# A state-space layer beside attention with memory rows: V of the memory rows turned by transposing DMA instead of TensorE

## The chip, the cores and the metric

The kernel runs on one core of one Trainium2 chip. Times are microseconds (us) of device time of one execution; the median of three executions is given. The profile was taken by the hardware profiler on one execution; its span runs from the first to the last instruction.

## The reference

Two independent layers read a sequence of 2048 tokens with 1024 features each, and their outputs are put side by side. Part A is a diagonal complex state-space recurrence. Part B is attention over segments of 32 tokens, 64 segments one after the other; each segment sees 8 memory rows, which are the output of the segment before.

```python
for s in range(n_seg):                                   # 64 segments
    h = jnp.concatenate([mem, x[:, s*32:(s+1)*32]], axis=1)   # 8 memory rows and 32 tokens
    q, k, v = (einsum('btd,dhe->bhte', h, W) for W in (Wq, Wk, Wv))   # 32 heads of 128
    p = softmax(where(mask, einsum('bhqe,bhke->bhqk', q, k) * scale, -1e9))
    o = einsum('bhte,hed->btd', einsum('bhqk,bhke->bhqe', p, v), Wo)
    mem, out = o[:, :8], o[:, 8:]
```

## The kernel before, in words

The segments of part B depend on each other only through the memory rows. The kernel guesses those rows (method `guess`), computes all segments at once with them, and checks at the end that the guess was good enough; if not, a slow exact loop (`general`) runs. So there are 73 memory rows beside the 2048 tokens: NM = 73, of which NMX = 7 belong to the first segment and NTL = 66 to the others.

The work goes through four stages.

1. **Stage one** (lines 999 to 1061). `warm` (line 960) issues short TensorE matmuls on zeros while the first data arrive. `v_x` (line 464) makes V = x Wv of the tokens, 512 tokens and four heads (a block, `hb`, of eight) at a time, and stores it to the DRAM tensor `b_vx`; for the first 512 tokens, x comes as rows and is turned by TensorE (`turn_x0`, line 404), whose results DVE or ACT copies out of PSUM. Part A's recurrence (`stage1`) is interleaved with it. In this stage the instructions of TensorE and of SP's queue stand in the written order (`k.pin`, line 1001).
2. **Stage two** (lines 1067 to 1093). Part A's output product, 32 halves of a tile of 128 tokens, 16 matmuls of 512 columns each, counted by `i`. Between the halves `guess` runs (until `i` = 23), and then the first two steps of `v_mem` (line 541), for blocks 0 and 1. SP's queue is still in the written order.
3. **Attention** (lines 1096 to 1135). For 16 pairs of heads, `proj` makes Q and K of a pair in 18 steps (16 matmuls of 201 columns for the odd columns in each of two steps, 8 of 480 columns in each of sixteen), and `attention` takes 11 units a pair: scores (`psS`), exponential on ACT, mask on GpSimd, the product with V (`psO` or `psR`, from `att_back`) and the division on DVE. LEAD = 10 projection steps run before the first unit, and the rest is spread between the units. The compiler may reorder here, except where `keep_in_program_order` is called. The steps of `v_mem` for blocks 2 to 7 run at units 4 and 6 of every second pair.
4. **Output product** and the check.

`v_mem` for block `hb` multiplies Wv (the tile `b_wv`, two buffers; the next load of Wv waits until the matmuls are done with the old one) by the 73 guessed rows, which gives V of these rows with the head's 128 features on the partitions (`b_vm`). It has to stand the other way, rows on the partitions. So four TensorE transposes turn it, DVE copies it into a staging tile `b_vst` (line 555), and SP stores 7 rows to `b_vx` and 66 rows to `b_vt` in DRAM (lines 557 and 558). Each head has 128 columns of V and then columns of ones, which give the softmax's sum.

`load_v` (line 619) brings V of a pair of heads from `b_vx` and `b_vt` into one of two buffers `b_v`. For the first two pairs it first fills 29 partitions (rows 99 to 127) with zeros from DRAM, by a DMA of 22 x 29 pieces. The load for pair 0 is issued by `att_init` (line 690), the load for pair hp + 1 at unit 2 of pair hp. Lines 625 and 627 keep the zeros and the body in program order on SP.

Of the kernel before, what the change touches and what calls it, by code (L numbers as in the profile page):

```python
# [9 lines left out]
BF16 = mybir.dt.bfloat16  # L10
# [16 lines left out]
HB = 8; HP = 16  # L27
# [7 lines left out]
NMX = 7  # L35
NM = NTL + NMX
# [3 lines left out]
EW = E + 8  # L40
# [13 lines left out]
class Pinned:  # L54


    def __init__(self, k, name, eng):
        self.k, self.name, self.eng = k, name, eng
# [278 lines left out]
class PartB:  # L337
    def __init__(self, k, x, mem0, Wq, Wk, Wv, Wo, out):
        self.k = k
        self.x, self.mem0, self.out = x, mem0, out  # L340
        self.Wf = [w.rearrange("(c p) h e -> p c (h e)", p=128) for w in (Wq, Wk, Wv)]
        self.Wo = Wo.rearrange("h e d -> e h d")
        self.vx = [k.drp.tile([NSLOT, 4 * EW], BF16, name=f"b_vx{i}") for i in range(HB)]
        self.vt = [k.drp.tile([NTL, 4 * EW], BF16, name=f"b_vt{i}") for i in range(HB)]
        self.on = [k.drp.tile([T, 1024], BF16, name=f"b_on{i}") for i in range(4)]
        self.tn = [k.drp.tile([NR, 1024], BF16, name=f"b_tn{i}") for i in range(4)]
        c = k.cst
        self.m0T = c.tile([128, KC, M], BF16, name="b_m0T")
        self.gx = c.tile([128, KC, NM], BF16, name="b_gx")
        self.vmp = c  # L350
        self.xbar = c.tile([128, KC, NSEG], BF16, name="b_xbar")
        self.ogT = c.tile([128, H, NSEG], BF16, name="b_ogT")
        self.accE = c.tile([128, HP * NU], FP32, name="b_accE")
        self.accR = c.tile([128, HP * 2 * NG], FP32, name="b_accR")
        self.flag = c.tile([1, 1], I32, name="b_flag")
# [48 lines left out]
    def turn_x0(self, i):  # L404

        k = self.k
        pt = k.ps("U", (128, 2, KC, 128), BF16)[:, 0, :, :]
        for c in range(KC):
            k.PE.transpose(pt[:, c, :], self.x0[i][:, c * 128:(c + 1) * 128], k.ident[:])
        k.copy("vs"[i // 2], self.xe[:, :, 128 * i:128 * i + 128], pt)  # L410

    def sum_x(self, tmp):

# [50 lines left out]
    def v_x(self, hb, q, w):  # L464

        k = self.k
        Q = k.nc.scalar
        vx = self.vx[hb]
        st = self.next_st()
        first = hb == 0 and q == 0  # L470
        if first:

            ps = [k.ps("P")[:] for _ in range(3)]
            self.turn_x0(0)
            k.warm(6)
            self.turn_x0(1)
            for i, c in ((0, 0), (0, 1), (1, 0), (1, 1)):
                self.v_mm(ps[i], w, i, 128 * c, 128 * c + 128)
            self.turn_x0(2)
            self.v_mm(ps[0], w, 0, 256, 512)  # L480
            self.v_mm(ps[1], w, 1, 256, 512)
            self.turn_x0(3)
            ps.append(k.ps("U", (128, 2, 512))[:, 0, :])
            self.v_mm(ps[2], w, 2)
            self.v_mm(ps[3], w, 3)
        for i in range(4):
            if first:
                p = ps[i]
            else:
                p = k.ps("P")[:]  # L490
                self.v_mm(p, w, 4 * q + i)
            k.copy("v" if first and i % 2 else "s", st[:, i, :, 0:E], p.rearrange("p (h e) -> p h e", h=4))
        s0 = GX + 4 * q * 128
        n = 4 if q < 3 else 3
        Q.dma_start(vx[s0:s0 + n * 128, :].rearrange("(i p) n -> p i n", p=128), st[:, 0:n, :, :].rearrange("p i h e -> p i (h e)"))
        if q == 3:
            sv = st[:, 3, :, :].rearrange("p h e -> p (h e)")
            Q.dma_start(vx[0:64, :], sv[0:64, :])
            Q.dma_start(vx[T - 32:T + 32, :], sv[64:128, :])
# [41 lines left out]
    def v_mem(self, hb, w=None):  # L541
        k = self.k
        w = w or self.load_wv(hb)
        p = k.ps("P")
        for h in range(4):
            for c in range(KC):
                k.PE.matmul(p[:, h * NM:(h + 1) * NM], w[:, c, h * 128:(h + 1) * 128], self.memT[:, c, :], start=(c == 0), stop=(c == KC - 1))
        vm = self.vmp.tile([128, 4, NM], BF16, name="b_vm", bufs=1)
        k.copy("v", vm[:], p[:, 0:4 * NM].rearrange("p (h n) -> p h n", h=4))
        yield  # L550
        pt = k.ps("P", (128, 1024), BF16)
        for h in range(4):
            k.PE.transpose(pt[0:NM, h * 128:(h + 1) * 128], vm[:, h, :], k.ident[:])
        st = self.next_st()
        k.copy("v", st[0:NM, 0, :, 0:E], pt[0:NM, 0:512].rearrange("p (h e) -> p h e", h=4))
        sv = st[:, 0, :, :].rearrange("p h e -> p (h e)")
        k.SP.dma_start(self.vx[hb][64:64 + NMX, :], sv[0:NMX, :])
        k.SP.dma_start(self.vt[hb][:], sv[NMX:NM, :])
        yield


# [397 lines left out]

def warm(k, pool):  # L960

    w = pool.tile([128, 128], BF16, name="a_n", bufs=1)
    k.V.memset(w[:], 0.0)
    p = k.ps("R")

    def more(n):
        for _ in range(n):
            k.PE.matmul(p[:, 0:128], w[:], w[:], start=True, stop=True)
    more(24)
    k.warm = more  # L970


def hint(k):
# [6 lines left out]
def kernel_main(tc, A_x, A_Lre, A_Lim, A_Bre, A_Bim, A_Cre, A_Cim, A_logdt, A_Dskip, B_x, B_mem0, B_Wq, B_Wk, B_Wv, B_Wo, out,  # L980
                force=False, dbg=None):
    with ExitStack() as ctx:
        k = K(tc, ctx)
# [3 lines left out]
        b = PartB(k, B_x, B_mem0, B_Wq, B_Wk, B_Wv, B_Wo, out)  # L987

        def pool(name, side, bufs=2):
            return tc.tile_pool(name=name, bufs=bufs, side=side, reuse_waits="tile")  # L990
# [8 lines left out]
        with pool("p1x", "right") as p1x, pool("p1", "right", 1) as p1:  # L999
            a.tab = a.tmp = a.wp = a.btp = p1  # L1000
            k.pin |= {"PE", "SP"}
            warm(k, p1)
            w0 = b.wl.tile([128, KC, 512], BF16, name="b_wv", bufs=2)
            b.load_wv_part(w0, 0, 0, 128, nc.scalar)
# [5 lines left out]
            wv = {0: w0, 1: b.load_wv(1)}  # L1010
# [17 lines left out]
            for kind, pc, q in order[1:]:  # L1028
# [3 lines left out]
                if kind == "v":  # L1032
                    b.v_x(pc, q, wv[pc])
                    if q == 3:
                        if pc >= 3:
                            b.og(pc, wv[pc])
                        n = (pc + 2) if pc + 2 < PC else (2, 0)[pc + 2 - PC]
# [3 lines left out]
                n = 4 * pc + q  # L1041
# [27 lines left out]
        with pool("p2h", "right") as p2h, pool("p2", "right") as p2:  # L1069
            a.s2_tiles(p2h, p2)  # L1070
            g = b.guess(p2)
            s2 = a.stage2()
            b.wog = []
            a.load_h(1, nc.scalar)
            for i, _ in enumerate(s2):
                if i in (1, 4, 7):
                    n = (2, 0, 1)[(i - 1) // 3]
                    b.og(n, wv[n], "O")
                    if n == 2:
                        wv[1] = b.load_wv(1)  # L1080
                if i in (3, 7, 11, 15):
                    b.load_wog((3, 7, 11, 15).index(i), p2)
                if i in (9, 11, 13, 15, 17, 19, 21, 22):
                    next(g)
                if i == 20:
                    b.load_wqk(0)
                if i == 23:
                    for _ in g:
                        pass
                if i in (26, 28):  # L1090
                    vm = b.v_mem((i - 26) // 2, wv[(i - 26) // 2])
                if 26 <= i < 30:
                    next(vm)


# [15 lines left out]
        for n, (hp, u) in enumerate(at):  # L1111
            if n == 12:
                k.SP.dma_start(wo0[:], b.Wo[:, :, 0:512])
            if hp % 2 == 0 and 2 < hp + 2 < HP:
                if u == 4:
                    vm = b.v_mem(hp // 2 + 1)
                if u in (4, 6):
                    next(vm)
            if hp == 13 and u in (3, 6, 9):
                b.load_o_early(u // 3 - 1)  # L1120
            want = min(18 * HP, LEAD + (n + 1) * 18 // 11)
            while done < want:
                next(pr)
                done += 1
            if done == 18 * HP:
                if first is None:
                    xs.close()
                    b.p4a = ctx.enter_context(pool("p4a", "left", 1))
                    wo1 = b.p4a.tile([128, H, 512], BF16, name="wo1")
                    b.wo = (wo0, wo1)  # L1130
                    b.load_o_early(3)
                    for h in range(0, H, 16):
                        k.SP.dma_start(wo1[:, h:h + 16, :], b.Wo[:, h:h + 16, 512:D])
                    first = b.outproj_first()
                next(first)
# [90 lines left out]
```

## Time and profile before

| what | value |
|---|---|
| median of three executions | 1248.39 us (1248.22 to 1248.77) |
| the profiled execution | 1248.77 us |
| its span, first to last instruction | 1247.0 us |
| instructions | 20164 |
| mean granted TensorE clock | 1.000 |
| SP's DMA queue | 147.95 MB, 293830 packets |

How to read the lines that follow in this document. A group line gives the line of the kernel (often that of a helper, L64 for all TensorE and SP calls), the engine, the operation, what it writes and reads by the program's names (`psP<-b_xe,b_wv` is a matmul into a PSUM tile of tag P that reads `b_xe` and `b_wv`), its shape, how many there are, and durations in ns (least, median, largest). A timeline line gives start and length in us of a run of like instructions. `SPq` is SP's queue of DMA issues; its length is the time in which the instruction is being issued, not the transfer. A piece of the chain of waits gives the start, the length and what the end of the program hung on at that time.

### The profile page before, as it was taken

How to read it: one execution, taken by the hardware profiler on the slowest of the kernel's cores; microseconds unless marked ns; L12 is line 12 of the kernel's file. 1: busy time of each engine (PE TensorE's matmuls, PEld its weight loads, DVE VectorE, ACT ScalarE, POOL GpSimd, SP SyncE). 2: the span in 40 equal slices, each digit the busy share in tenths (PEclk: the TensorE clock that was granted, in tenths of full speed). 3: DMA queues.
4: the chain of work that ended last, by engine and by line, in shares of the span. 5: the costliest groups of instructions: out<-in, count | busy, mean ns of one | idle time of the engine just before them, and what ended most of it. 6: DMA issues, size and time to landing. Idle time of an engine off the chain costs nothing.

```text
span 1247.0 us, 20164 instructions
## 1 busy us (share of the span) xinstructions
PE 1235.0 (99%) x8292; PEld 664.7 (53%) x8364; DVE 667.9 (54%) x1250; ACT 263.4 (21%) x631; POOL 275.8 (22%) x407
## 2 busy tenths in 40 slices
PE   9999999999999999999999999999999999999998
PEld 5444444444455555656566656555665554446444
DVE  4688899998711124666666666666666641001000
ACT  5344344443310000211111111111211110000000
POOL 4111331222322321222222222322222320000000
PEclk9999999999999999999999999999999999999999
DMA  9975444554898834665454544545374289407000
GB/s 239 248 210 160 130 121 134 148 150 113 232 322 248 258 113 97 176 181 120 100 144 108 144 108 112 139 90 133 94 156 97 59 224 218 112 18 153 17 17 27
DMA packets 316022, 176.83 MB, mean 142 GB/s; under 512 B 138650, under 2 KB 301326, under 8 KB 315926
## 3 DMA queue, kind: packets, MB, share of 16 engines
q1 hardware_dynamic: 293830, 147.95, 48.4%
q10 hardware_dynamic: 21072, 24.38, 5.9%
q0 software_dynamic: 1024, 3.17, 0.7%
q8 instruction: 66, 1.08, 0.4%
q14 instruction: 30, 0.25, 0.1%
HBM read 89.14 MB, written 53.17 MB: 114 GB/s over the span
## 4 chain that ended last, share of the span: by engine, by line
PE 97%; DMA 2%; ACT 1%; issue 0%; POOL 0%; DVE 0%; ACTq 0%
PE psP L64 81%; PE psU L64 9%; PE psS L64 3%; PE psO L64 2%; PE psR L64 2%; DMA b_vx<-b_vst 1%; DMA wo<-in_B_Wo_dram 1%; DMA b_xr<-in_B_x_dram 0%; ACT b_vst L89 0%; ACT L187 0%; POOL b_m L645 0%; ACT a_fr L236 0%; ACT a_k L233 0%; ACT a_k L229 0%; ACT a_tabf L231 0%
## 5 line engine op out<-in xcount | busy, mean ns | idle before, releaser
L64 PE MATMUL psP<-b_xe,b_wq 128*128 128x480 bf16 (+1 forms) x1280 | 247.7, 343 | 0.1
L64 PE MATMUL psP<-b_xe,b_wk 128*128 128x480 bf16 (+1 forms) x1280 | 247.7, 343 | 0.0
L64 PE MATMUL psP<-b_wv,b_xe 128*128 128x512 bf16 (+2 forms) x1033 | 223.6, 373 | 1.6 <-ACT b_vst L89 0.9
L645 POOL TENSOR_TENSOR b_m<-b_e,maskB 99x396 bf16<-99x396 bf16 x160 | 139.8, 874 | 334.3 <-ACT b_e L642 334.3
L642 ACT ACTIVATE b_e<-psS 99x396 bf16<-99x396 f32 x176 | 88.2, 501 | 532.5 <-PE psS L64 528.2
L64 PEld LDWEIGHTS <-b_wk 128*128 128x128 bf16 x1280 | 119.4, 98 | 94.2
L64 PEld LDWEIGHTS <-b_xe 128*128 128x128 bf16 x1056 | 102.2, 98 | 119.8 <-issue 1.3
L64 PEld LDWEIGHTS <-b_wq 128*128 128x128 bf16 x1280 | 118.7, 98 | 87.7
L91 DVE CAST b_k<-psP 128x480 bf16<-128x480 f32 (+1 forms) x192 | 97.5, 529 | 101.3 <-PE psP L64 101.3
L91 DVE CAST b_q<-psP 128x480 bf16<-128x480 f32 (+1 forms) x192 | 97.5, 529 | 92.9 <-PE psP L64 91.3
L64 PEld LDWEIGHTS <-b_ol 128*128 128x128 bf16 x864 | 84.3, 98 | 94.4
L64 PE MATMUL psU<-a_xT,a_bt 128*128 128x512 bf16 x493 | 113.9, 379 | 1.1
L64 PE MATMUL psP<-t,a_hl 128*128 128x512 bf16 x496 | 112.1, 379 | 0.8
L91 DVE CAST b_ost<-psP 128x512 bf16<-128x512 f32 (+1 forms) x17 | 11.5, 676 | 183.4 <-PE psP L64 182.4
L64 PE MATMUL psP<-wo,b_ol 128*128 128x512 bf16 (+1 forms) x440 | 91.9, 364 | 0.4
L64 PE MATMUL psP<-t,b_ol 128*128 128x512 bf16 x408 | 91.7, 379 | 0.4
L280 POOL TENSOR_SCALAR a_tt<-a_pr,a_tabf 128x1 f32<-128x1 f32 x48 | 34.0, 709 | 244.5 <-DVE a_pr L275 244.5
L89 ACT ACTIVATE b_vst<-psP 128x512 bf16<-128x512 f32 x126 | 72.1, 589 | 70.3 <-PE psP L64 61.3
L662 DVE TENSOR_TENSOR b_ob<-psO,b_accR 99x384 bf16<-99x384 f32 x160 | 85.9, 553 | 2.0
L267 DVE TENSOR_TENSOR a_pr<-psU,a_tabf 128x2048 f32<-128x2048 f32 x32 | 73.0, 2283 | 14.8 <-PE psU L64 13.1
L64 PEld LDWEIGHTS <-a_bt 128*128 128x128 bf16 x512 | 49.2, 98 | 57.6
L64 PEld LDWEIGHTS <-a_hl 128*128 128x128 bf16 x512 | 49.1, 98 | 56.6
(200 smaller groups left out, 966.3 us busy)
## 6 DMA issues: line engine op xcount, KB each, us to landing
b_v<-b_vx SPq DMA_DIRECT2D x16, 1122.0 KB
b_wv<-in_B_Wv_dram SPq DMA_DIRECT2D x16, 1024.0 KB
b_on<-b_ob SPq DMA_DIRECT2D x15, 960.0 KB
b_vx<-b_vst ACTq DMA_DIRECT2D x24, 544.0 KB
a_hs<-a_h SPq DMA_DIRECT2D x32, 256.0 KB
b_wog<-in_B_Wo_dram SPq DMA_DIRECT2D x4, 2048.0 KB
b_wq<-in_B_Wq_dram SPq DMA_DIRECT2D x16, 512.0 KB
b_wk<-in_B_Wk_dram SPq DMA_DIRECT2D x16, 512.0 KB
```

What stands on the lines that cost most here:

```text
L64: r = f(*a, **kw)
L89: self.S.activation(out, in_, ACT.Copy)
L91: self.V.tensor_copy(out, in_)
L267: V.tensor_tensor(pr[:], u[:].unsqueeze(1).to_broadcast([128, 2, 2, TB]), view(t3, [[TB + 1, 2], [TB + 1, 2], [1, TB]]), ALU.mult)
L280: G.tensor_scalar(tt[:, j:j + 1], w[:, j, TB - 1:TB], t3[:, 1, TB:TB + 1], None, ALU.mult)
L642: k.S.activation(e[:], s[0:GW, :, :, 0:GW], ACT.Exp, scale=float(E) ** -0.5, accum_out=self.accE[0:GW, i:i + 1])
L645: k.G.tensor_tensor(m[0:GW, 0:4 * GP].rearrange("p (a b q) -> p a b q", a=2, b=2)[:, :, :, 0:GW], e[:], mask[0:GW, :, :].unsqueeze(2).to_b ...
L662: V.tensor_tensor(self.ob[:, b0:b0 + n, :], o[0:GW, 0:n, 0:E], r.unsqueeze(2).to_broadcast([GW, n, E]), ALU.mult)
```

## The change

Three things are changed.

- **The turn of the memory rows.** `b_vm` becomes one tile of 128 columns a head, with zeros in columns 73 to 127. After the cast, SP stores it to a new DRAM tensor `b_vmt` (4 heads x 128 x 128). In a second step four transposing DMAs on SP read it back, turned, into the staging tile (now with 144 columns a head), and DVE sets the columns of ones. In a third step SP makes the two stores to `b_vx` and `b_vt`, as before.
- **Where the steps stand.** Blocks 0 and 1 have their three steps after halves 25 to 27 and 28 to 30 of stage two, in place of two steps after 26, 27 and 28, 29. Blocks 2 to 7 have them at units 4, 6 and 8.
- **The start.** The warm-up is 8 matmuls of 512 columns, in place of 24 of 128 and 6 more between the first two turns of x. The copies of the four turned pieces of x go to DVE, ACT, DVE, ACT, in place of DVE, DVE, ACT, ACT.

```diff
@@ __init__ of PartB
+        self.vmt = [k.drp.tile([4, E, 128], BF16, name=f"b_vmt{i}") for i in range(HB)]
@@ turn_x0
-        k.copy("vs"[i // 2], self.xe[:, :, 128 * i:128 * i + 128], pt)
+        k.copy("vs"[i % 2], self.xe[:, :, 128 * i:128 * i + 128], pt)
@@ v_x
             self.turn_x0(0)
-            k.warm(6)
             self.turn_x0(1)
@@ v_mem, after the matmuls
-        vm = self.vmp.tile([128, 4, NM], BF16, name="b_vm", bufs=1)
-        k.copy("v", vm[:], p[:, 0:4 * NM].rearrange("p (h n) -> p h n", h=4))
+        if hb == 0:
+            self.vm = self.vmp.tile([128, 4, 128], BF16, name="b_vm", bufs=1)
+            k.V.memset(self.vm[:, :, NM:128], 0.0)
+        k.copy("v", self.vm[:, :, 0:NM], p[:, 0:4 * NM].rearrange("p (h n) -> p h n", h=4))
+        k.SP.dma_start(self.vmt[hb].rearrange("h e n -> e h n"), self.vm[:])
         yield
-        pt = k.ps("P", (128, 1024), BF16)
+        s = self.next_st()[:].rearrange("p i h e -> p (i h e)")[:, 0:576].rearrange("p (h e) -> p h e", h=4)
+        k.V.memset(s[:, :, E:EW], 1.0)
         for h in range(4):
-            k.PE.transpose(pt[0:NM, h * 128:(h + 1) * 128], vm[:, h, :], k.ident[:])
-        st = self.next_st()
-        k.copy("v", st[0:NM, 0, :, 0:E], pt[0:NM, 0:512].rearrange("p (h e) -> p h e", h=4))
-        sv = st[:, 0, :, :].rearrange("p h e -> p (h e)")
-        k.SP.dma_start(self.vx[hb][64:64 + NMX, :], sv[0:NMX, :])
-        k.SP.dma_start(self.vt[hb][:], sv[NMX:NM, :])
+            k.SP.dma_start_transpose(s[:, h, 0:E], self.vmt[hb][h])
+        yield
+        k.SP.dma_start(self.vx[hb][64:64 + NMX, :].rearrange("n (h e) -> n h e", h=4), s[0:NMX, :, 0:EW])
+        k.SP.dma_start(self.vt[hb].rearrange("n (h e) -> n h e", h=4), s[NMX:NM, :, 0:EW])
         yield
@@ warm
-    w = pool.tile([128, 128], BF16, name="a_n", bufs=1)
+    w = pool.tile([128, 512], BF16, name="a_n", bufs=1)
     k.V.memset(w[:], 0.0)
     p = k.ps("R")
-
-    def more(n):
-        for _ in range(n):
-            k.PE.matmul(p[:, 0:128], w[:], w[:], start=True, stop=True)
-    more(24)
-    k.warm = more
+    for _ in range(8):
+        k.PE.matmul(p[:], w[:, 0:128], w[:], start=True, stop=True)
@@ kernel_main, stage two
-                if i in (26, 28):
-                    vm = b.v_mem((i - 26) // 2, wv[(i - 26) // 2])
-                if 26 <= i < 30:
+                if i in (25, 28):
+                    vm = b.v_mem((i - 25) // 3, wv[(i - 25) // 3])
+                if 25 <= i < 31:
                     next(vm)
@@ kernel_main, attention
-                if u in (4, 6):
+                if u in (4, 6, 8):
                     next(vm)
```

## The prediction

> **What bounds the kernel now.** I read the page from the top: busy times, then the chain that ended last.
>
> ```profile
> PE 1235.0 (99%) x8292; PEld 664.7 (53%) x8364; DVE 667.9 (54%) x1250; ACT 263.4 (21%) x631; POOL 275.8 (22%) x407
> PE 97%; DMA 2%; ACT 1%; issue 0%; POOL 0%; DVE 0%; ACTq 0%
> ```
>
> TensorE is busy for 1235.0 of 1247.0 us and is 97% of the chain: matmul time taken off it is won in full, and each hole put into it is paid in full. So I look for what the change removes from PE, and then for waits that come so close to it that a hole opens. First, by tile, the memory rows' operations:
>
> ```profile
> L64 PE MATMUL psP<-ident,b_vm x32: 219/219/219, 456.8 to 910.3; 128*73 128x128 bf16 x32
> L91 DVE CAST b_vm<-psP x8: 461/462/463, 453.6 to 904.9; 128x292 bf16<-128x292 f32 x8
> ```
>
> Next the timelines of PE and of SP's queue around the first two memory-row steps, up to the first attention product:
>
> ```profile
> 452.29 1.25 PE L64 MATMUL psP<-b_xe,b_wv 128*128 128x73 bf16 x32
> 453.38 3.62 PE L64 MATMUL psP<-t,a_hl 128*128 128x512 bf16 x15
> 456.83 0.39 PE L64 MATMUL psP<-ident,b_vm 128*73 128x128 bf16 x4
> 457.05 3.62 PE L64 MATMUL psP<-t,a_hl 128*128 128x512 bf16 x16
> 460.50 1.25 PE L64 MATMUL psP<-b_xe,b_wv 128*128 128x73 bf16 x32
> ...
> 493.59 0.50 PE L64 MATMUL psO<-b_v,b_m 128*128 128x129 bf16 x6
> ```
>
> ```profile
> 453.57 0.38 SPq L64 DMA_DIRECT2D b_wv<-in_B_Wv_dram  x1
> 458.07 0.30 SPq L64 DMA_DIRECT2D b_vx<-b_vst  x1
> 458.43 0.30 SPq L64 DMA_DIRECT2D b_vt<-b_vst  x1
> 461.78 0.41 SPq L64 DMA_DIRECT2D b_wv<-in_B_Wv_dram  x1
> 466.28 0.27 SPq L64 DMA_DIRECT2D b_vx<-b_vst  x1
> 466.60 0.29 SPq L64 DMA_DIRECT2D b_vt<-b_vst  x1
> 466.98 0.26 SPq L64 DMA_DIRECT2D b_v<-b_vt  x1
> 467.29 16.05 SPq L64 DMA_DIRECT2D b_v<-b_vx  x2
> ```
>
> Four transposes hold PE from 456.83 to 457.05, 0.22 us. And the last SP line is the point of the case. Right behind the memory rows' stores, SP issues the load of V for head pair 0: first zeros into 29 rows (22 x 29 pieces of 544 B, which run on one DMA engine at about 20 pieces per 0.5 us), then the body. The body's issue hangs for 15.7 us until the zeros are through. In the trace's semaphore records the body lands on fifteen engines from 490.16 to 491.12 and on the engine with the zeros at **493.50**. PE's sequencer waits for that semaphore from 490.30 to 493.53, and the first product with V starts at 493.59. The chain shows it as a small hole:
>
> ```profile
> 493.28 0.18 PE psS L64 x4
> 493.46 0.13 issue
> 493.59 0.50 PE psO L64 x6
> ```
>
> So this load has **no slack**: whatever delays its issue delays PE by the same time.
>
> **The change, part by part.**
>
> *Removed on PE:* 8 times 4 transposes. 8 x 0.22 = 1.76 us, all on the bounding engine. The two groups before 493 (0.44 us) only bring PE earlier to the wait for V; the six later ones (1.3 us) count in any case. On DVE each step loses a copy of 0.39 us and gains a memset of 32 columns (one of 50 takes 0.10 in the timeline); DVE is 54% busy, nothing.
>
> *Added on SP, per memory-row step:* one store of V's rows to DRAM, four transposing DMAs that wait for its landing, then the two old stores, which wait for the transposes instead of for DVE. All stand in SP's queue in written order in this stage (line 1001 pins SP until line 1096, and lines 625 and 627 pin the load of V). Prices:
> - The store: on an empty queue the two old stores take from 466.28 to 468.47 to land, 2.2 us. Behind a 1 MB load of Wv it must wait for it: that load takes 453.57 to 458.54, 5.0 us, and 1.1 us more for the store's own data.
> - A transpose of 128x128: no row shows one. The smallest issues in the trace (64x1024, 80x1024, 128x1024) take 1.27, 1.23 to 1.28 and 1.29 us; half the rows save 0.02, so I take the floor, a pitch of 1.31. Lower end 0.26, the shortest DMA issue on SP; upper end 1.31.
> - Landing of the last: the fourth transpose of the check's tile starts to issue at 1071.14 and has landed at 1073.94, 2.8 us (upper end 3.3, its third; lower end 2.2, the stores). Four in a row: 3 x 1.31 + 2.8 = 6.7 us.
>
> The Trainium skill speaks against the change here ("VectorE: DVE Perf Modes", section "The three transpose paths"): it has 390 ns for a 128x128 transpose on TensorE and 1309 ns for the DMA crossbar, and advises TensorE if PSUM will do. The rows above have 219 ns, of which 55 on PE's stream, and 1.23 to 1.31 us of issue alone; with 4 x 1.309 = 5.2 us a group in place of 6.7 the delay below would be 3 us shorter.
>
> *The sum for the load of V.* Memory rows 0 move up by half a token tile, 3.45 us: matmuls end at 453.54 - 3.45 = 450.1. The load of Wv for block 2 waits for the same matmuls and stands at the head of SP (as at 453.57), so it goes first and lands at 455.1. The store, ready after the 0.46 us cast, lands at 456.2; four transposes land at 462.9; the old stores issue until 463.6. Memory rows 1 stay: their matmuls end at 461.5, but SP is not free. Wv for block 3 goes at 463.7 and lands at 468.7, the store at 469.8, the transposes at 476.5, and two stores and the small load (0.30 + 0.35 + 0.30) bring the zeros to 477.5. Now they go at 467.29: **10.2 us later**. V lands at 503.7; PE stands there at 493.0 and waits. Net: +10.2 - 1.3 = **+8.9 us**. After that all that hangs on SP is late by the same time as PE, so nothing is paid twice: Wq for pair 1 has landed at 494.62 and is used at 503.24, V for pair 1 at 519.3 and 526.7.
>
> *Memory rows 2 to 7, inside attention:* stages now at units 4, 6 and 8 of a pair, two units (some 6 us) for each landing. With 6.1 us for a store behind a load of Wv and 6.7 for the turns, a group may hold SP for 12.8 us; behind it stand the stores of outputs and the weights of the next pair. Wk issued at 570.25 is wanted about 600, V issued at 560.5 about 593, and the rows themselves at the second next pair's load, a unit-8 store against unit 2 of the following pair, 5 units or 15 us. So 12.8 us are covered and cost nothing; were the cover gone, PE would wait for what sticks out, which rival 3 prices. The extra 2 MB on the DMA engines (142 GB/s in the mean) are nothing.
>
> *Warm-up and the start.* 128 columns are spaced 107 ns until the clock doubles at 7.10 us, so 512 columns should take 427 (estimate), eight 3.4 us, from 1.25 (longer memset) to 4.66 in place of 3.82; the first turn of x ends about 5.5. The second waits for its rows, landed at 5.68, and starts at 5.73 now: the six short matmuls only filled that wait. Its copy on ACT takes 1.02 in place of 0.69 us and costs PE some 0.2 us at 7.7; this dies in the 0.91 us hole at 34.39, where PE waits for a store that landed at 34.57. I take 0. Ends: -0.4 (the hole before the first turn, 0.36, is filled) and +2.1: were the clock to rise another 6.0 us later, half of that is lost, less the 0.9.
>
> On this the skill has a rule ("TensorE: Matmul & The Clock Gate", Part 4): transposes do not count as busy for the clock gate. By it, taking six matmuls from between the turns could put the rise off; the clock here rose at 7.10 after 1.7 us of transposes in the last 2.9, which neither shows nor excludes it. With the page's window of some 3.4 us at half clock the loss would be 1.7 us, 0.8 after the hole (an estimate).
>
> **The sum.** The profiled execution took 1248.77 us (span 1247.0 and 1.8 around it), the slowest of three, 0.4 above their median. 1248.8 + 8.9 = 1257.7, at the median's level **1257.4**.
>
> **Rivals.**
> 1. *Shorter queue on SP.* If the compiler puts the Wv loads behind the stores, the groups take 2.2 + 6.7 each: first group done at 460.2, second store at 462.0, zeros at 471.9, +4.6: net +3.3, 1251.7. With one load ahead (block 2's): 473.6, +6.3: 1253.4. With transposes at 0.26 and no load ahead the zeros go at 468.2, and all is even. For it: the store is written before the Wv load. Against: the load is ready 0.46 us earlier, and stands first in the trace of before.
> 2. *The other side: the wait is hidden.* PE is not pinned in attention (line 1061). If the compiler sees V late and puts projection steps (8 x 202 ns = 1.62 us each) in front of the first product, PE stays full; it needs six or seven steps for 10.2 us, and with fewer each takes 1.6 off. Then -1.76 alone is left: 1246.6. Against: PE's order in the trace of before follows the written one through the whole attention, 13 projection steps before it, though V came at the last moment.
> 3. *Attention's queue runs late too:* a late load once per two pairs, say six times 0.5 to 1 us on top: over 1260.5.
>
> **How the numbers follow.** Forecast (1255 to 1260 by itself) 0.42; rival 1 0.25; rival 2 0.25; rival 3 0.08. Rival 2 may not be left out of the range, rival 3 may: 1246.4 to 1260.5. About 0.2% (2.5 us) is what a measurement can tell from no change. Rival 2 lies within it but for 0.03 (start-up's gain on top), and rival 1 with the cheapest transposes adds 0.02: faster 0.03, same 0.24, slower 0.73.
>
> **What would show it.** Right: a hole of some 10 us in PE's timeline before the first psO<-b_v, the zeros' issue near 477, transposes of about 1.3 us in two groups of four after 455, no other new hole, attention and projection 1.3 us shorter. Wrong: zeros before 470 (rival 1 at its cheapest), PE full with 19 or more projection steps before the first product (rival 2), or holes at the heads of later pairs (rival 3).

## The result, and the profile after

| | median, us | least to largest | runs |
|---|---|---|---|
| before | 1248.31 | 1247.09 to 1248.77 | 4 |
| after | 1263.03 | 1262.38 to 1264.79 | 4 |

The change makes the kernel slower: the ratio after to before is 1.0122 (95% interval 1.0104 to 1.0139), 14.7 us. The prediction had the direction and the place, but its 1257.4 is 5.6 us short and its range ended at 1260.5. The profiled execution of after took 1262.38 us, with a span of 1260.7 us and a mean granted clock of 0.995 (before: 1.000).

The page of after, its first line and the shares of the chain of waits:

```profile
PE 1236.5 (98%) x8240; PEld 661.4 (52%) x8310; DVE 666.4 (53%) x1251; ACT 263.6 (21%) x631; POOL 275.7 (22%) x407
PE 93%; DMA 5%; SPq 1%; issue 0%; DVE 0%; POOL 0%; ACT 0%; ACTq 0%; DVEq 0%
```

TensorE is busy for as long as before, in a span that is 13.7 us longer. DMA and SP's queue have taken 4% more of the chain, so the loss is waiting for transfers. SP's queue over the first two memory-row blocks, as a timeline:

```profile
449.50 0.38 SPq L64 DMA_DIRECT2D b_wv<-in_B_Wv_dram  x1
450.00 0.63 SPq L64 DMA_DIRECT2D b_vmt<-b_vm  x1
...
455.62 4.98 SPq L64 DMA_TRANSPOSE b_vst<-b_vmt  x4
463.42 0.98 SPq L64 DMA_DIRECT2D b_vx<-b_vst  x1
464.44 0.85 SPq L64 DMA_DIRECT2D b_vt<-b_vst  x1
465.40 0.47 SPq L64 DMA_DIRECT2D b_wv<-in_B_Wv_dram  x1
468.60 0.39 SPq L64 DMA_DIRECT2D b_vmt<-b_vm  x1
472.81 4.96 SPq L64 DMA_TRANSPOSE b_vst<-b_vmt  x4
479.07 0.82 SPq L64 DMA_DIRECT2D b_vx<-b_vst  x1
479.94 0.83 SPq L64 DMA_DIRECT2D b_vt<-b_vst  x1
...
481.33 16.19 SPq L64 DMA_DIRECT2D b_v<-b_vx  x2
```

The reader is to see two chains of the same form, one behind the other: load of Wv, store, four turns, two stores. The gaps between the lines are waits for a landing (the one ahead of 468.60 is a wait for DVE). Each group of turns issues for 5.0 us, 1.24 each. The zeros of V for head pair 0 (last line) go at 481.33; in the kernel before they went at 467.29, so they are 14.0 us later. The chain of waits shows what that does:

```profile
481.69 25.76 DMA b_v<-b_vx
507.45 0.14 issue
507.58 0.57 PE psO L64 x6
```

The body of the load lands 26.1 us after the zeros are issued (before: 26.2), and the first product follows at once. PE's timeline up to that product has three holes (in brackets, with what ended each), where the kernel before had one of 0.1:

```profile
468.63 3.61 PE L64 MATMUL psP<-t,a_hl 128*128 128x512 bf16 x16 [0.81 <-DVE b_vm L91]
...
484.61 3.15 PE L64 MATMUL psP<-b_xe,b_wq 128*128 128x480 bf16 x8 [7.98 <-DVE b_q L91]
487.60 3.40 PE L64 MATMUL psP<-b_xe,b_wk 128*128 128x480 bf16 x16
...
507.58 0.57 PE L64 MATMUL psO<-b_v,b_m 128*128 128x129 bf16 x6 [4.71 <-DMA b_v<-b_vx]
507.95 3.41 PE L64 MATMUL psP<-b_xe,b_wk 128*128 128x480 bf16 x8
```

Two things here were not in the prediction. The first is that the two holes in front are waits for **DVE**, not for V. DVE's timeline says why:

```profile
468.05 0.09 DVE L555 MEMSET b_vst<- 128x32 bf16 x1 [7.43 <-DMA b_vt<-b_vst]
...
482.83 0.09 DVE L555 MEMSET b_vst<- 128x32 bf16 x1 [9.86 <-DMA b_vt<-b_vst]
```

These set the columns of ones for blocks 2 and 3. They are written in attention, but DVE's order is not pinned, and the compiler has put them into stage two. The staging tiles are those of blocks 0 and 1, so each memset waits until that block's rows have landed in DRAM, and the copies out of PSUM wait behind it on DVE. The second is the length of the matmuls after the holes: 8 projection matmuls take 3.15 and 3.41 us there, and 16 take 3.40 elsewhere. In the trace's records the granted clock is 0.5 from 480.58 to 487.40 and from 507.88 to 511.30.

### The profile page after: what moved, and what is told of

It is laid out like the page before. It is cut to its first block, busy times and chain, and to the rows that moved or that the text cites. A ratio compares the mean times of both kernels' runs of the same rounds, so it can differ in the third digit from the quotient of the medians.

```text
span 1260.7 us, 20102 instructions
## 1 busy us (share of the span) xinstructions
PE 1236.5 (98%) x8240; PEld 661.4 (52%) x8310; DVE 666.4 (53%) x1251; ACT 263.6 (21%) x631; POOL 275.7 (22%) x407
## 4 chain that ended last, share of the span: by engine, by line
PE 93%; DMA 5%; SPq 1%; issue 0%; DVE 0%; POOL 0%; ACT 0%; ACTq 0%; DVEq 0%
PE psP L64 77%; PE psU L64 9%; PE psS L64 3%; PE psO L64 2%; DMA b_v<-b_vx 2%; PE psR L64 2%; SPq L64 1%; DMA b_vmt<-b_vm 1%; DMA wo<-in_B_Wo_dram 1%; DMA b_wv<-in_B_Wv_dram 1%; DMA b_vst<-b_vmt 0%; DMA b_vt<-b_vst 0%; DVE b_vm L91 0%; POOL b_m L647 0%; DVE b_ost L91 0%
```

## The experiments

Before was run beside them: 1247.96 us for the first four, 1248.36 for the others.

| kernel | median, us | least to largest | ratio to before, 95% |
|---|---|---|---|
| 1 new start only | 1247.23 | 1246.84 to 1247.68 | 0.9986 to 1.0005 |
| 2 after, ones once | 1263.73 | 1262.25 to 1264.07 | 1.0108 to 1.0141 |
| 3 after, zeros by GpSimd | 1256.69 | 1255.68 to 1257.40 | 1.0053 to 1.0086 |
| 4 after, both | 1245.05 | 1244.82 to 1245.38 | 0.9969 to 0.9988 |
| 5 before, queue delayed | 1254.91 | 1254.27 to 1256.38 | 1.0034 to 1.0068 |
| 6 before, new start, zeros by GpSimd | 1247.29 | 1246.92 to 1247.72 | 0.9983 to 1.0002 |
| 7 after, ones once, loads of Wv later | 1254.62 | 1253.89 to 1255.32 | 1.0035 to 1.0069 |
| 8 after, blocks 0 and 1 by TensorE | 1244.88 | 1244.59 to 1245.36 | 0.9962 to 0.9982 |

The theory is that SP's queue delays the load of V, which has no slack. Its rival, after the trace, is DVE's memsets: behind them wait the copies for which PE stands 8 us.

**1. The start alone.** Before, with the new warm-up and the new copies of x's pieces.

> The kernel before with the new start alone (8 warm-up matmuls of 512 columns, none between the turns of x, copies on DVE and ACT in turn); V of the memory rows is turned as before. All theories that put the loss near the first attention product expect no loss here. In the profile after, the matmuls of the second stage-one group began 0.45 us later than before (15.65 against 15.20), but the first state-space matmuls 0.6 us earlier (36.41 against 37.02), since the wait at 34.39 went: 1247.7, between 1247.2 and 1248.6. Were the start the cause: 1255 or more.

Measured 1247.23, 0.7 below before, with an interval that holds no change. In after's trace the hole of 0.91 us at 34.39 is gone. The start costs nothing.

**2. The ones once.** DVE's memset is left out where the tile already holds the ones.

```diff
-        k.V.memset(s[:, :, E:EW], 1.0)
+        if hb < 2:
+            k.V.memset(s[:, :, E:EW], 1.0)
```

> The changed kernel, but DVE sets the columns of ones in the staging tiles only for blocks 0 and 1; nothing overwrites them later. This takes away the two memsets that waited on DVE until 468.05 and 482.83, and with them the 0.8 and 8.0 us holes of PE at 467.8 and 476.6. Queue theory (the load of V for head pair 0 stands behind the memory rows' chain on SP, and the holes lie in the shadow of that wait): the zeros go at 480 to 481 in place of 481.3, PE's holes become one wait of 12 to 13 us before the first product, time 1261 to 1263.5. DVE theory (the memsets' waits are the loss): 1253 to 1255.

Measured 1263.73, a little over the 1261 to 1263.5 expected: nothing is won. The rival, as the one cause, is out. PE's timeline at the first product:

```profile
509.03 0.81 PE L64 MATMUL psO<-b_v,b_m 128*128 128x129 bf16 x6 [16.12 <-DMA b_v<-b_vx]
```

The busy times by windows; the columns are the window, its length, the busy time of PE, PEld, DVE, ACT and POOL with their instructions, the granted clock, the DMA share and GB/s:

```profile
492.90:509.00 16.10, 0.01 (x1) 0.01 (x1) 0.53 (x1) 0.59 (x2) 0.87 (x1) 0.59 0.68 145
509.00:513.00 4.00, 3.97 (x19) 2.04 (x20) 1.27 (x4) 0.00 (x0) 0.00 (x0) 0.53 0.08 23
```

The 8 us hole is gone and one of 16.12 us stands in front of V (12 to 13 were expected): PE does nothing in the first window, while the DMA engines are busy for 68% of it. The zeros go at 482.84 (480 to 481 were expected), no earlier than in after. So the memset of block 2 had not held them up either: the store of block 1 is issued 2.1 us earlier here, at 466.53, and lands at 473.29, where it landed at 472.75 in after; kernel 7 shows what it waits for. The four us after the hole run at a clock of 0.53.

**3. The zeros by GpSimd.** The zeros go into the buffers without a DMA, so that nothing hangs in front of the body. (A load of Wo in attention is kept in program order as well.)

```diff
-                z = self.vx[0][T + 32:T + 32 + 128 - GW, 0:2 * EW].unsqueeze(1).to_broadcast([128 - GW, NG, 2 * EW])
-                k.tc.keep_in_program_order(k.SP.dma_start(vt[GW:128, :, :], z))
+                k.G.memset(vt[GX:128, :, :], 0.0)
```

> The changed kernel, but the 29 rows of zeros of V's buffers are set by GpSimd instead of a DMA on SP in front of the load, and the load of Wo's first half is held in the written order so that it does not slip in front of V. V's body can land some 7 us after its issue at about 481, near 488. Queue theory alone: no wait left, 1246.5 to 1247.5. DVE theory alone: no change, 1262 to 1264. Both, one in the shadow of the other: the wait for V goes, the 8 us hole of DVE's memset comes out of the shadow, and half-clock time after it: 1255.5 to 1258.5.

Measured 1256.69. PE's timeline at the hole, and at the first product with V:

```profile
484.96 3.38 PE L64 MATMUL psP<-b_xe,b_wq 128*128 128x480 bf16 x8 [8.17 <-DVE b_q L91]
...
504.57 0.50 PE L64 MATMUL psO<-b_v,b_m 128*128 128x129 bf16 x6
```

V is in time now, the first product waits for nothing, and the wait for DVE is paid alone. Against kernel 4, below, it costs 11.6 us: the holes of 0.58 and 8.17 us, and half of the 5.9 us (484.96 to 490.82) at a clock of 0.5, make 11.7. So after holds two waits, each of which hides most of the other; that is why taking away DVE's alone, in 2, gave nothing.

**4. Both.**

> Both edits of the two kernels above on the changed kernel. Queue theory, and both overlapping: nothing is left to wait for before the first product, 32 TensorE transposes less than before, 1245.5 to 1247. DVE theory alone: 1253 to 1255 as with the first edit. If the staging chains of blocks 2 to 7 inside attention cost something of their own, it is left here: above 1248.

Measured **1245.05**, half a us under the range expected, ratio 0.9979 (0.9969 to 0.9988): a little faster than the kernel before, and 18 us faster than after. SP's queue and PE's first product:

```profile
480.40 0.52 SPq L64 DMA_DIRECT2D b_v<-b_vx  x1
480.96 1.87 SPq L64 DMA_DIRECT2D b_v<-b_vt  x1
```

```profile
492.48 0.50 PE L64 MATMUL psO<-b_v,b_m 128*128 128x129 bf16 x6
```

The queue is as late as in after, and the body is issued at 480.40. With no zeros in front of it, it lands at 489.97, 2.5 us before the product that wants it. All of the loss is thereby taken away by two edits that do not touch the turn.

**5. The delay without the change.** Before, where the store of block 1's 66 rows is issued four times, each time after the landing of the one ahead.

```diff
-        k.SP.dma_start(self.vt[hb][:], sv[NMX:NM, :])
+        for _ in range(4 if hb == 1 else 1):
+            k.SP.dma_start(self.vt[hb][:], sv[NMX:NM, :])
```

> The kernel before, with nothing of the change in it, but the store of block 1's 66 rows to DRAM is issued four times; each further one waits for the landing of the one ahead of it (about 2.2 us each), and the zeros and the body of V for head pair 0 stand behind them in SP's queue. No slack (my theory): the zeros are issued 6 to 7 us later than at 467.3, one hole opens before the first product with V, and the time is 1248 + 6 to 7, with up to 1.7 more if the granted clock falls behind the hole: 1254 to 1256.5. Rival (the load of V has slack that the trace does not show, and the loss after the change has another cause): 1248.

Measured 1254.91, 6.6 above before. SP's queue, and PE's first product:

```profile
467.36 3.75 SPq L64 DMA_DIRECT2D b_vt<-b_vst  x3
471.20 0.25 SPq L64 DMA_DIRECT2D b_v<-b_vt  x1
472.51 0.28 SPq L64 DMA_DIRECT2D b_vt<-b_vst  x1
472.85 16.31 SPq L64 DMA_DIRECT2D b_v<-b_vx  x2
```

```profile
498.91 0.81 PE L64 MATMUL psO<-b_v,b_m 128*128 128x129 bf16 x6 [4.70 <-DMA b_v<-b_vx]
```

The zeros are 5.6 us later, the product 5.3; from the product to the end of the span it takes 755.8 us in place of 753.4, and the clock is 0.5 until 503.95, 5.04 us behind the product, half of which is 2.5. This execution is the slowest of its four, 1.5 us above their median; its hole in the start, ahead of 36.05, is 1.77 us where before's is 0.91, and its mean clock is 0.997 where the other three have 0.998 to 0.999. That the load has no slack is shown; the price behind the hole is shown for this execution.

**6. A control for 4.** The zeros by GpSimd and the new start in the kernel before, with TensorE's turns.

> The kernel before with the new start, and the zeros of V's buffers set by GpSimd instead of by DMA; the memory rows are turned by TensorE. A control for the run with both edits (1245.05). If those 2 us under the new start alone (1247.23) come from the 32 transposes that are gone, this takes 1247.0 (1246.7 to 1247.5). If they come from the zeros, 1245.1.

Measured 1247.29: without the DMA turn, setting the zeros by GpSimd gives nothing. The 2.2 us between 6 and 4 go with the turn by DMA.

**7. The loads of Wv out of the way.** As 2, with the two 1 MB loads for blocks 2 and 3 moved into attention.

```diff
+            if n == 4:
+                k.pin.add("SP")
+                wvx = {m: b.load_wv(m) for m in (2, 3)}
+                k.pin.remove("SP")
...
-                    vm = b.v_mem(hp // 2 + 1)
+                    vm = b.v_mem(hp // 2 + 1, wvx.pop(hp // 2 + 1, None))
```

> The changed kernel with the columns of ones set only for blocks 0 and 1, and with the two loads of Wv (1 MB each, blocks 2 and 3) held back into attention, so that they no longer stand in front of the memory rows' stores on the way to DRAM. If stores waiting behind these loads make a good part of the delay: zeros issued near 474 in place of 482.8, time 1253.6 to 1255.5. Rival (the store, turn and store chain alone makes the delay, the loads run beside it): 1261 or more.

Measured 1254.62, 9.1 below kernel 2. SP's queue:

```profile
450.19 0.40 SPq L64 DMA_DIRECT2D b_vmt<-b_vm  x1
...
452.19 4.97 SPq L64 DMA_TRANSPOSE b_vst<-b_vmt  x4
...
461.63 0.41 SPq L64 DMA_DIRECT2D b_vmt<-b_vm  x1
464.17 4.96 SPq L64 DMA_TRANSPOSE b_vst<-b_vmt  x4
...
472.68 16.39 SPq L64 DMA_DIRECT2D b_v<-b_vx  x2
```

A store now lands 2.0 and 2.5 us after its issue; right behind a load of Wv it took 5.5 us in after (450.00 to 455.55), and 6.8 in kernel 2 (466.53 to 473.29). The zeros go 10.2 us earlier than in kernel 2. Against the kernel with the new start alone (466.14) they are 6.5 late: that is what the turns and stores by themselves cost, and the rest of the delay is the two loads that stand in front of small stores. One hole is left:

```profile
499.30 0.81 PE L64 MATMUL psO<-b_v,b_m 128*128 128x129 bf16 x6 [6.72 <-issue]
```

V landed at 499.21, so this too is the wait for V.

**8. Only attention's rows by DMA.** Blocks 0 and 1 are turned by four TensorE transposes and a copy as before, at halves 26 to 29 (left out in the diff); blocks 2 to 7 by DMA (their ones set by GpSimd).

```diff
-        if hb == 0:
+        if hb < 2:
...
+        if hb == 2:
```

> The changed kernel, but the memory rows of blocks 0 and 1 are turned by TensorE and copied, at the halves where the kernel before has them; blocks 2 to 7, inside attention, are turned by DMA. The load of V for pair 0 is then issued as early as before. If the turn by DMA costs nothing inside attention: 1247.2 less 24 transposes of 55 ns, 1245.9 (1245.4 to 1246.6). If the chains on SP's queue cost something in attention: over 1247.5.

Measured **1244.88**, a us better than expected and below the range. From the first to the last product with V it takes 522.84 us; with the new start alone it takes 524.21, and in kernel 4 522.85. So the 24 turns in attention give 1.36 us, as their 24 x 55 ns say, and attention's queue costs nothing. The other 1.0 lies behind the last store of the output: from its issue to the end of the span it takes 4.28 to 4.39 us in the four kernels without a DMA turn in attention, and 3.30 to 3.75 in the six with one. SP's last drain ends 0.6 to 1.0 us after the start of the instruction ahead of it in the four, and 0.08 in the six; why, stays open.

## Why the prediction was wrong

**Right** (in brackets, what the prediction took). *The place and the mechanism*: the load of V for pair 0 has no slack (5), the chain on SP delays it, PE stands in front of the first product, and V lands 26.1 us after its zeros are issued. *The order*: Wv goes first, ahead of the store, so rival 1 is out. PE's order is the written one in after too, so rival 2 is out. No hole opens at a later pair, and kernel 8 shows that attention's turns are free, so rival 3 is out; the time lies above 1260.5, where rival 3 stood, but for the reasons below. *The turns*: 1.24 us of issue each (taken 1.31), and 5.0 + 2.7 and 5.0 + 1.2 us a group to the landing (taken 6.7). *The gain*: 1.36 us in attention (taken 1.3).

**Wrong, the sum for the load of V.** The zeros were to go 10.2 us later and went 14.0 later. Term by term, where after's chain stands against the predicted one (plus is late):

| term | predicted | after | late so far |
|---|---|---|---|
| first store landed | 456.2 | 455.55 | -0.65 |
| first turns landed | 462.9 | 463.27 | +0.4 |
| next load of Wv issued | 463.7 | 465.40 | +1.7 |
| second store landed | 469.8 | 472.75 | +2.95 |
| second turns landed | 476.5 | 478.92 | +2.4 |
| zeros issued | 477.5 | 481.33 | +3.8 |

The mis-sized terms are the stores and the loads of Wv. The stores were priced by their old rows, 0.30 and 0.35 us of issue. In after they have four pieces of 272 B a row where one row was one piece, and take 0.98 + 0.85 and 0.82 + 0.83 us: that is the step of 1.3 from the second row to the third and, with the small load (0.47 in place of 0.30), the step of 1.4 to the last. The loads of Wv take 5.7 and 6.7 us to land in place of 5.0, and the second makes the step to the fourth row; why it takes longer, stays open. The chain began 0.6 us early (449.50 in place of 450.1), which hid part of this. The 1.1 us for a store's own data behind a load had no run behind it: after's stores landed 0.4 and 0.7 us behind the loads.

**Wrong, the clock behind a hole.** "PE stands there at 493.0 and waits" was priced at the wait alone. The clock is halved behind it: 507.88 to 511.30 at 0.5 is 3.4 us, of which half, 1.7, is lost; from the first to the last product with V after takes 524.52 us and kernel 4, without the hole, 522.85. The rule was at hand in the Trainium skill, "TensorE: Matmul & The Clock Gate", Part 1: after an idle window of some 3.4 us the array goes to half clock until a busy window has passed, and the windows run on by themselves. The runs agree: all six holes from 4.70 to 16.12 us brought a clock of 0.5, those of 0.58, 0.81 and 1.77 did not, and the stretches last 3.41, 6.83, 10.24 and 17.07 us, multiples of 3.41. Past the start, no run has a hole between 1.8 and 4.7 us.

**Wrong, "DVE is 54% busy, nothing".** DVE's busy time was right, but its order was not thought of: the memset of ones needs the staging tile, and waits at the head of DVE's queue for two stores to land. In after this is hidden by the wait for V (2), but without that wait it costs 11.6 us (3). The sign "no other new hole" failed here.

**The sum of it.** For the profiled execution 1257.7 was predicted and 1262.38 came: +3.8 for the zeros, +1.7 for the clock, -0.6 for the end (3.74 us behind the last store's issue in place of 4.36), and -0.2 that I do not assign. Against kernel 4's span of 1243.5 after's 1260.7 is 17.2 more: holes of 0.81 + 7.98 + 4.71 = 13.5, half clock behind the first long hole (484.61 to 487.40) 1.4 and behind the second 1.7, and the end 0.4, 17.0 in all.

**The start** was taken as 0 and measured as -0.7, within the uncertainty.

## What to carry to other kernels

A few tenths taken off the bounding engine are lost when they are paid for with a chain on a queue that a load without slack stands behind: follow the queue to the next load that the bounding engine waits for, and count every landing in between, large loads that stand in front of small stores above all. A hole long enough to halve the clock (here from 4.7 us on) cost 1.4 to 2.9 us behind it as well. Where two waits overlap, taking away one shows nothing; take away both before a cause is dropped.

## What the runs showed of the hardware

- A store of the same rows takes 0.82 to 0.98 us to issue in pieces of 272 B (28 and 264 pieces), and 0.27 to 0.30 in whole rows (7 and 66).
- A 128 x 128 transposing DMA from DRAM holds SP's queue for 1.1 to 1.2 us (27 of 32 in after; the other five, in attention, 1.4 to 2.9); the last of a group of four lands 2.3 to 3.8 us after it starts to issue (478.92 and 463.27 in after).
- A store of 128 KB issued right behind a 1 MB load on the same queue lands 5.5 to 6.8 us after its issue (after, kernels 2 to 4), and 2.0 to 2.5 without the load (kernel 7).
- The zeros for 29 rows, 638 pieces on one DMA engine, hold the issue of the next load on that queue for 15.6 to 16.0 us, and it lands 26 us after them; without them the same load landed 7.8 to 9.8 us after its issue (kernels 3, 4 and 6).
